# A fixed order for the opening and the first block of a linear-attention and two-MLP kernel

## The chip, the cores and the metric

The program runs on one core of a Trainium2 chip. The metric is the device time of one execution in microseconds (us), here the median of three runs. Engines are named as the profile names them: PE (TensorE, matmuls), DVE (VectorE), ACT (ScalarE), POOL (GpSimd), and SP, whose queue issues all DMAs of this kernel. Each engine carries out its own instructions strictly in the order in which they were built and waits on semaphores for the others.

## What is computed

Three stages follow each other: a gated linear attention over 4 batches, 8 heads, 768 tokens and 48 features per head, an MLP with a sigmoid gate, and an MLP with `h - tanh(h)`. Each MLP takes 3072 tokens from 384 features to 2048 and back.

```python
def _attn_ref(q, k, v, alpha):
    B, H, S, D = q.shape
    state = np.zeros((B, H, D, D), dtype=np.float32)
    y = np.zeros_like(q)
    for t in range(S):
        state = alpha[:, :, t, :, None] * state + np.einsum('bhd,bhe->bhde', k[:, :, t], v[:, :, t])
        y[:, :, t] = np.einsum('bhd,bhde->bhe', q[:, :, t], state)
    return y.astype(np.float32)
def _moe_ref(x, w_in, w_out):
    h = x @ w_in
    g = h * (1.0 / (1.0 + np.exp(-1.702 * h)))
    return (g @ w_out).astype(np.float32)
def _moe2_ref(x, w_in, w_out):
    h = x @ w_in
    g = h - np.tanh(h)
    return (g @ w_out).astype(np.float32)
```

The weights arrive as 64-bit floating-point numbers, and the kernel turns them into pairs of 32-bit numbers itself.

## The kernel before

**Attention** is done in 24 chunks of 128 tokens, numbered g, six per batch. For one chunk:

- `a_load(g)`: four DMAs (five for chunk 0) bring decay factors, keys, queries and values, 1.1 MB, into `arena` (chunks take turns in two places; chunk 2 has a third one in `gt` and `xs`).
- `prep(g, 0..3)`: two scans on DVE (L237) with a reciprocal between them, two multiplications that scale keys and queries (L243, L244), and a square of the decay factors on ACT that serves a guard (`a_guard`, L248). The square overwrites what it reads.
- `a_scores(g, x)`: eight score matmuls in two halves (L273), copied from the PSUM banks by ACT (L278, L286) and masked by POOL (L283, for chunks under `FULL` = 8).
- `a_out(g)`: eight matmuls with the carried state (L302), eight with the values (L305), eight for the new state (L312), then the state's update on DVE (L316 to L319).
- `a_evac(g)`: ACT copies the result y from PSUM to `ys` (L326), four DMAs write it to `xt` in DRAM (L331), one DMA reads it back with features on the partitions (`xlo`, L332), ACT rounds it to `xhi` (L333), and DVE (POOL from chunk 8 on) subtracts to leave the low half in `xlo` (L334).

**The MLPs** work in blocks of 512 tokens, six for each layer, with 16 steps m in a block, one for each 128 hidden features. Step s does nine matmuls into a hidden bank (`gemm1`, L343: three 128-feature parts, each as high x high, low x high and high x low), the activation (for layer 1 a tanh on ACT, L357, and a DVE instruction, L358, together `sig_1`), the split of the result into `ghi` (ACT, L361) and `glo` (DVE or POOL, L362), and three steps later nine matmuls into the output banks (`gemm2`, L350). Two hidden banks are used in turn. Block 0 needs the y of chunks 0 to 3. During each layer-1 block the chunks of the next block are worked off (`attend`).

**The weights** of layer 1 are 16 tiles of 768 KB. For each, `w_load` is one DMA into one of three `raw` buffers; `w_bits` is two DVE instructions (L160, L161), `w_join` one (L173), and `w_split` is an ACT cast to `whi` (L190) and a DVE subtraction to `wlo` (L191). `conv(1)` does a split, a join and a pair of bits for three successive tiles, and the join sets off the load of the tile three further on. There are five buffers `cf`/`xs` for tiles between bits and split.

**What sets the order.** The code is written out in one order, but the tile framework puts the instructions of each engine into an order of its own, by dependencies and by its own reckoning of times. In the opening the code calls all four parts of chunks 0 to 3 and three `conv(1)`; in block 0 each step calls `gemm1`, `sig_1`, `g_split` of the step before, the due parts of `attend` and one `conv(1)`. What runs when, DVE's order of weight conversions and chunk work above all, is the framework's choice.

## Time and profile before

| | us |
|---|---|
| median of 3 runs (lowest 973.59, highest 977.31) | 974.5 |
| the profiled execution, its own time | 975.3 |
| its span from first to last instruction | 973.2 |
| PE busy (share of the span) | 940.9 (97%) |
| DVE busy | 606.0 (62%) |
| ACT busy | 460.6 (47%) |
| POOL busy | 191.7 (20%) |

PE is near full over the whole span, but the page's 40 slices of 24.3 us show that its first four are not (5, 9, 6 and 8 tenths), while DVE is at 7, 9, 8 and 9 tenths in them and the DMA engines at 9, 7, 9 and 5. The table is read by stage: the opening up to the first MLP matmul, block 0, and the rest. The difference of 2.1 us between the execution's own time and its span lies around the first and the last instruction.

### The profile page before, as it was taken

The page shows a single profiled execution, that of the slowest core. Times are in us where ns is not written, and L with a number is a line of the kernel's source. Part 1 is how long each engine was busy: PE and PEld are TensorE (multiplying, and loading weights), DVE is VectorE, ACT ScalarE, POOL GpSimd, SP SyncE. Part 2 cuts the span into 40 slices and gives each one's busy share as a digit, 9 for nine tenths or more (in the row PEclk, how much of TensorE's full clock was granted, in tenths as well). Part 3 has the DMA queues.
Part 4 walks back from the last instruction along what each step waited for, and adds up shares of the span by engine and source line. Part 5 has one row for each costly group of instructions (what it writes and reads, how often), then busy time and mean ns, then how long its engine had stood idle before and what let it go on. Part 6 is the DMA issues. An engine that isn't in the chain of part 4 may idle for free.

```text
span 973.2 us, 13227 instructions
## 1 busy us (share of the span) xinstructions
PE 940.9 (97%) x4870; PEld 739.7 (76%) x4870; DVE 606.0 (62%) x914; ACT 460.6 (47%) x969; POOL 191.7 (20%) x150
## 2 busy tenths in 40 slices
PE   5968999999999999999999999999999999999997
PEld 4646787777777777777788888888888888888885
DVE  7989742442343453453339996766777777766663
ACT  4445434333443534434344555554556656545542
POOL 1222202434434434334230110100100101000000
PEclk9999999999999999999999999999999999999999
DMA  9795221432445463761324330100233420000001
GB/s 282 245 305 166 85 53 28 131 92 67 137 141 153 151 205 116 247 196 41 92 71 158 134 130 1 65 33 0 70 126 98 161 100 0 33 1 1 33 0 37
DMA packets 58043, 101.84 MB, mean 105 GB/s; under 512 B 4992, under 2 KB 37376, under 8 KB 57968
## 3 DMA queue, kind: packets, MB, share of 16 engines
q1 hardware_dynamic: 57968, 100.90, 32.6%
q8 instruction: 40, 0.66, 0.3%
q14 instruction: 35, 0.29, 0.1%
HBM read 86.73 MB, written 14.16 MB: 104 GB/s over the span
## 4 chain that ended last, share of the span: by engine, by line
PE 87%; DMA 5%; DVE 5%; issue 1%; ACT 1%; SPq 0%; POOL 0%; DVEq 0%; ACTq 0%
PE bank L350 40%; PE bank L343 40%; DMA arena<-xq 4%; PE bank L273 3%; PE bank L305 2%; DMA raw<-w 2%; DVE arena L237 1%; PE bank L302 1%; PE bank L312 1%; DVE cf L161 1%; DVE cf L173 1%; DVE wlo L191 0%; DVE cf L160 0%; DVE xs L173 0%; ACT arena L248 0%
## 5 line engine op out<-in xcount | busy, mean ns | idle before, releaser
L343 PE MATMUL bank<-xhi,whi 128*128 128x512 f32 x576 | 230.0, 400 | 0.2 <-ACT xhi L333 0.2
L343 PE MATMUL bank<-xlo,whi 128*128 128x512 f32 x576 | 229.8, 399 | 0.0
L343 PE MATMUL bank<-xhi,wlo 128*128 128x512 f32 x576 | 229.0, 398 | 0.0
L350 PE MATMUL bank<-ghi,whi 128*128 128x512 f32 x576 | 229.0, 398 | 0.0
L350 PE MATMUL bank<-ghi,wlo 128*128 128x512 f32 x576 | 228.5, 397 | 0.0
L350 PE MATMUL bank<-glo,whi 128*128 128x512 f32 x576 | 223.8, 396 | 0.0
L361 ACT CAST ghi<-gt 128x512 fp32r<-128x512 f32 x192 | 119.0, 620 | 199.2 <-DVE gt L373 124.1
L358 DVE SCALAR_TENSOR_TENSOR gt<-gt,bank 128x512 f32<-128x512 f32 x96 | 65.5, 682 | 125.8 <-ACT gt L357 122.7
L362 DVE TENSOR_TENSOR glo<-gt,ghi 128x512 fp32r<-128x512 f32 x128 | 93.2, 728 | 79.4 <-ACT ghi L361 76.0
L343 PEld LDWEIGHTS bank<-xhi,whi 128*128 128x128 f32 x576 | 109.0, 189 | 27.4 <-issue 1.6
L343 PEld LDWEIGHTS bank<-xlo,whi 128*128 128x128 f32 x576 | 109.1, 189 | 26.2 <-issue 1.4
L343 PEld LDWEIGHTS bank<-xhi,wlo 128*128 128x128 f32 x576 | 109.2, 190 | 25.7 <-issue 0.6
L350 PEld LDWEIGHTS bank<-ghi,whi 128*128 128x128 f32 x576 | 108.5, 188 | 26.4 <-issue 1.2
L350 PEld LDWEIGHTS bank<-ghi,wlo 128*128 128x128 f32 x576 | 108.5, 188 | 25.4 <-issue 0.8
L350 PEld LDWEIGHTS bank<-glo,whi 128*128 128x128 f32 x576 | 108.3, 188 | 25.1 <-DVE arena L243 0.2
L362 POOL TENSOR_TENSOR glo<-gt,ghi 128x512 fp32r<-128x512 f32 x64 | 85.8, 1341 | 139.0 <-ACT ghi L361 127.8
L410 POOL TENSOR_TENSOR xlo<-arena,xhi 128x512 fp32r<-128x512 f32 x18 | 27.9, 1574 | 307.6 <-ACT xhi L409 307.6
L357 ACT ACTIVATE gt<-bank 128x512 f32<-128x512 f32 x96 | 57.1, 595 | 64.0 <-PE bank L343 63.1
L237 DVE TENSOR_TENSOR_SCAN arena<-arena,seg 112x516 f32<-112x516 f32 x46 | 62.8, 1365 | 35.4 <-DMA arena<-xq 34.7
L371 DVE SCALAR_TENSOR_TENSOR arena<-arena,bank 128x512 f32<-128x512 f32 x96 | 65.7, 685 | 30.4 <-ACT arena L369 29.7
L369 ACT ACTIVATE arena<-bank 128x512 f32<-128x512 f32 x96 | 57.3, 597 | 42.2 <-PE bank L343 41.9
L373 DVE SCALAR_TENSOR_TENSOR gt<-arena 128x512 f32<-128x512 f32 x96 | 68.3, 711 | 9.4
(85 smaller groups left out, 853.7 us busy)
## 6 DMA issues: line engine op xcount, KB each, us to landing
raw<-w SPq DMA_DIRECT2D x64, 768.0 KB, 4.7
arena<-xq SPq DMA_DIRECT2D x46, 224.0 KB, 3.0
arena<-xq SPq DMA_DIRECT2D x22, 451.5 KB, 5.8
xt<-arena SPq DMA_DIRECT2D x96, 48.0 KB, 3.0
xlo<-xt SPq DMA_DIRECT2D x24, 192.0 KB, 4.1
x1t<-xs SPq DMA_DIRECT2D x6, 768.0 KB, 5.2
arena<-x1t SPq DMA_DIRECT2D x6, 768.0 KB, 4.6
out<-xs SPq DMA_DIRECT2D x18, 256.0 KB, 2.3
```

The costliest lines, as they stand in the source:

```text
L237: V.tensor_tensor_scan(out=dec(g, n), data0=src(g, n), data1=seg, initial=0.0, op0=ALU.mult, op1=ALU.max)
L273: P.matmul(out=o[hh][:, i], lhsT=k[r, 2 * x + i], rhs=q[r, 2 * x + i], start=True, stop=True)
L343: P.matmul(out=h, lhsT=w[m][:, ws], rhs=x[:, k, :n], start=c == 0, stop=c == 3 * KT - 1)
L350: P.matmul(out=acc[k][:, :n], lhsT=w[m][:, ws], rhs=x[s % 3][:, :n], start=m == 0 and c == 0, stop=m == MT - 1 and c == 2)
L357: A.activation(out=th[i][:, :n], in_=h, func=AF.Tanh, scale=0.851)
L358: V.scalar_tensor_tensor(out=gf[i][:, :n], in0=th[i][:, :n], scalar=1.0, in1=h, op0=ALU.add, op1=ALU.mult)
L361: A.copy(ghi[s % 3][:, :n], gf[s % 2][:, :n])
L362: e.tensor_tensor(out=glo[s % 3][:, :n], in0=gf[s % 2][:, :n], in1=ghi[s % 3][:, :n].bitcast(F32), op=ALU.subtract)
L369: A.activation(out=u, in_=h, func=AF.Square, accum_out=usum[:, s - NS1 :][:, :1])
L371: V.scalar_tensor_tensor(out=p, in0=u, scalar=P3, in1=h, op0=ALU.mult, op1=ALU.mult)
L373: V.scalar_tensor_tensor(out=gf[i], in0=w, scalar=PD, in1=p, op0=ALU.add, op1=ALU.mult)
L410: G.tensor_tensor(out=xlo[i][:, k], in0=xr[:, k], in1=xhi[i][:, k].bitcast(F32), op=ALU.subtract)
```

## The change

The opening is written out by hand, block 0 is rewritten in the same way, and `in_order`, called after the last step of block 0, ties every instruction of an engine to the one in front of it in the code, so that the framework keeps the written order for all that was built up to there. From block 1 on the code and its ordering are as before. Within the written order:

- Loads: values of chunk 0 come behind the decay factors of chunk 1, both first weight tiles behind the loads of chunk 2, and each later chunk load behind the y writes of the chunk that freed its place. `conv` no longer issues a weight load itself: it notes it in `due`, and `fetch()` issues it at a chosen place.
- The y of even and odd chunks goes through two buffers (`ysb`; the second shares storage with `wt`, which the weight check uses later). The read-back of y (`a_back`) stands behind the y writes of the next chunk in the opening; the rounding and subtraction (`a_x`) come a chunk or more later.
- Chunks 0 to 3 have score banks 5, 6 and 3, 4 and output banks 0, 1, which are cleared at the start; the matmuls with the carried state come behind those with the values (chunks 0 to 3).
- In the opening five tiles get their bits, four their join and three their split. In block 0 a step calls `gemm1`, one `conv(1)`, the split of `g` of the step before, a part of a chunk (a chunk takes three steps), and then `sig_1`. The guard's square comes one step later.

```diff
+        early = g < L1[0][1] // C
+        if c and not early:
+            carried(True)
         for p, hh in heads:
...
+        if c and early:
+            carried(False)
...
+    def a_back(g):
+        _, xl, o = a_at(g)
+        tk = slice(g * C, g * C + C)
         SP.dma_start(out=xl[:, :, o].bitcast(F32), in_=xt.rearrange("h d t -> (h d) t")[:, tk].rearrange("(k p) t -> p k t", p=128))
...
+    def fetch():
+        while due:
+            w_load(*due.pop(0))
...
             if m + 3 < MT:
-                w_load(layer, m + 3)
+                due.append((layer, m + 3))
...
+    def a_done(g, b=5):
+        a_evac(g, b)
+        if g + 2 < NG:
+            a_load(g + 2)
+        if g < FULL:
+            a_back(g)
...
+    def in_order(since):
+        last = {}
+        for ins in nc.cur_bb.bb.instructions[since:]:
+            if ins.engine in last:
+                tc.add_manual_dep(ins, last[ins.engine], mybir.DependencyInfo(
+                    mybir.DependencyClass.NoSync, mybir.DependencyReason.DATA), reason="in_order")
+            last[ins.engine] = ins.name
...
+    for g in range(4):
+        if g > 1:
             conv(1)
+        for r in range(2):
+            a_scores(g, r, (5, 3)[r])
+        if g < 3:
+            for r in range(3):
+                prep(g + 1, r)
+        else:
+            prep(4, 0)
+            prep(4, 1)
+        if g == 1:
+            conv(1)
+        if g > 1:
+            a_x(g - 2)
+        a_guard(g)
+        a_out(g, 0)
+        a_state(g)
+        a_evac(g, 0)
+        if g == 0:
+            a_load(3)
+            w_load(1, 2)
+        if g:
+            a_back(g - 1)
+        fetch()
+        if g == 1:
+            a_load(4)
+    a_back(3)
+    conv(1)
+    a_x(2)
+    a_x(3)
+    fetch()
+    a_load(5)
+    conv(1)
+    prep(4, 2)
+    prep(4, 3)
...
             gemm1(i, m, h, n)
-            if l == 1:
+            if l == 1 and j:
                 sig_1(s, h, n)
-            else:
+            elif l == 1:
+                conv(1)
+                fetch()
+            if l == 2:
                 tanh_near(s, h)
...
             if l == 1 and j == 0:
-                conv(1)
+                sig_1(s, h, n)
+                if m % 3 == 2 and m < 12:
+                    a_done(m // 3 + 4)
+                    a_state(m // 3 + 4)
+                if m % 3 == 0 and 0 < m < 13:
+                    prep(m // 3 + 4, 3)
+                if m % 3 == 1 and m > 3:
+                    a_x(m // 3 + 3)
...
+        if s == MT - 1:
+            in_order(begin)
```

Three places show what the table of calls does to the engines. In the rows a line number, the operation, the tile written and the tiles read stand in this order; the number behind `wlo`, `whi` or `bank` is that of the weight tile or bank, and the one behind the underscore tells nothing.

DVE before, the seven instructions up to the fourth subtraction of L334 (chunk 3), which completes the input of block 0; the split of weight tile 6 among them is the ninth split so far:

```order
L161 SCALAR_TENSOR_TENSOR cf0_101<-raw1_96,cf0_101 128x768
L237 SCALAR_TENSOR_TENSOR arena_122<-arena_122,seg_123 112x516
L191 TENSOR_TENSOR wlo6_85<-cf1_102,whi6_69 128x768
L173 SCALAR_TENSOR_TENSOR cf0_101<-raw1_96,cf0_101 128x768
L316 TENSOR_TENSOR state_121<-bank7_131,state_121 112x192
L244 TENSOR_TENSOR arena_122<-arena_122 112x4x128
L334 TENSOR_TENSOR xlo0_106<-xlo0_106,xhi0_104 128x3x128
```

DVE after, the same place, where the subtraction is L364 and stands for chunks 1, 2 and 3, the split is L192, the join L174, the bits L161 and L162:

```order
L364 TENSOR_TENSOR xlo0_105<-xlo0_105,xhi0_103 128x3x128
L333 TENSOR_TENSOR state_120<-bank7_130,state_120 112x192
L334 TENSOR_TENSOR state_120<-state_120,arena_121 112x192
L192 TENSOR_TENSOR wlo1_80<-cf1_101,whi1_64 128x768
L174 SCALAR_TENSOR_TENSOR cf2_102<-raw2_97,cf2_102 128x768
L161 TENSOR_SCALAR xs_114<-raw0_95 128x768
L162 SCALAR_TENSOR_TENSOR xs_114<-raw0_95,xs_114 128x768
L364 TENSOR_TENSOR xlo0_105<-xlo0_105,xhi0_103 128x3x128 x2
L192 TENSOR_TENSOR wlo2_81<-cf2_102,whi2_65 128x768
```

Two splits (tiles 0 and 1) now stand ahead of that subtraction instead of nine, three joins and four pairs of bits; the rest moved behind it, into block 0.

DVE before, from the first `sig_1` of block 0 (L358) to the first `glo` (L362):

```order
L358 SCALAR_TENSOR_TENSOR gt_108<-gt_108,bank3_127 128x512
L161 SCALAR_TENSOR_TENSOR xs_115<-raw1_96,xs_115 128x768
L191 TENSOR_TENSOR wlo11_90<-cf1_102,whi11_74 128x768
L244 TENSOR_TENSOR arena_122<-arena_122 112x4x128
L236 MEMSET seg_123 112x4
L191 TENSOR_TENSOR wlo9_88<-xs_115,whi9_72 128x768
L358 SCALAR_TENSOR_TENSOR gt_108<-gt_108,bank4_128 128x512
L173 SCALAR_TENSOR_TENSOR xs_115<-raw1_96,xs_115 128x768
L362 TENSOR_TENSOR glo0_112<-gt_108,ghi0_109 128x512
```

DVE after, from the first `sig_1` (L388) to the second; `glo` is L392, the scan L241:

```order
L388 SCALAR_TENSOR_TENSOR gt_107<-gt_107,bank3_126 128x512
L192 TENSOR_TENSOR wlo4_83<-xs_114,whi4_67 128x768
L174 SCALAR_TENSOR_TENSOR cf0_100<-raw2_97,cf0_100 128x768
L161 TENSOR_SCALAR cf1_101<-raw0_95 128x768
L162 SCALAR_TENSOR_TENSOR cf1_101<-raw0_95,cf1_101 128x768
L392 TENSOR_TENSOR glo0_111<-gt_107,ghi0_108 128x512
L241 SCALAR_TENSOR_TENSOR arena_121<-arena_121,seg_122 112x516
L388 SCALAR_TENSOR_TENSOR gt_107<-gt_107,bank4_127 128x512
```

Before, tiles 9 and 11 were split next to the first `sig_1`; now it is tile 4, and each step of block 0 has one split, one join, one pair of bits, one `glo`, a part of a chunk and one `sig_1`.

SP's queue before, from the y writes of chunk 0 (L331) to the read-back of chunk 1 (the second L332); L153 is a weight load, L230 to L232 are chunk loads:

```order
L331 DMA xt_133<-arena_122 48x2x128 x4
L153 DMA raw1_96<-w1 128x1536
L230 DMA arena_122<-xq 112x512
L231 DMA arena_122<-xq 112x4x128
L153 DMA raw2_97<-w1 128x1536
L332 DMA xlo0_106<-xt_133 128x3x128
L331 DMA xt_133<-arena_122 48x2x128 x4
L232 DMA arena_122<-xv 128x384
L332 DMA xlo0_106<-xt_133 128x3x128
```

SP's queue after, from the load of weight tile 2 (L154) to the read-back of chunk 1 (the second L359); y writes are L346, chunk loads L230 to L236:

```order
L154 DMA raw2_97<-w1 128x1536
L346 DMA xt_132<-wtb_98 48x2x128 x4
L359 DMA xlo0_105<-xt_132 128x3x128
L230 DMA arena_121<-xq 112x1032
L232 DMA arena_121<-xq 112x512
L234 DMA arena_121<-xq 112x4x128
L236 DMA arena_121<-xv 128x384
L346 DMA xt_132<-arena_121 48x2x128 x4
L359 DMA xlo0_105<-xt_132 128x3x128
```

Before, two weight loads and half a chunk load stand between the y writes of chunk 0 and their read-back. Now the y writes of the next chunk stand directly in front of each read-back, and a whole chunk load follows it ahead of the next y writes; the weight tile stands in front of them.

## Rows read from the trace of the kernel before

**Rows 1.** Windows by stage: busy us (instructions) of each engine, PE clock, DMA share, GB/s.

```profile
0.00:65.50 65.50, 46.33 (x304) 34.34 (x305) 57.29 (x86) 29.17 (x79) 14.20 (x14) 1.00 0.89 274
65.50:108.24 42.74, 38.41 (x196) 27.01 (x197) 41.46 (x60) 20.38 (x47) 10.59 (x6) 0.92 0.54 166
108.24:150.35 42.11, 42.11 (x227) 33.19 (x226) 21.88 (x35) 16.74 (x36) 3.66 (x4) 1.00 0.22 62
150.35:973.20 822.85, 814.03 (x4146) 645.17 (x4144) 485.32 (x735) 394.28 (x809) 163.22 (x126) 1.00 0.28 90
```

**Rows 2.** Timeline of PE: start us, us, engine, line, operation, tiles, shapes, count [idle before].

```profile
8.72 4.05 PE L273 MATMUL bank<-arena 48*128 48x176 f32 x16 [8.72 <-ACT arena L218]
...
62.33 1.11 PE L302 MATMUL bank<-arena,state 48*48 48x128 f32 x16 [1.73 <-DVE state L317]
...
65.50 1.03 PE L343 MATMUL bank<-xhi,whi 128*128 128x512 f32 x2 [0.18 <-ACT xhi L333]
...
71.52 0.63 PE L343 MATMUL bank<-xhi,wlo 128*128 128x512 f32 x1
71.94 0.63 PE L343 MATMUL bank<-xlo,whi 128*128 128x512 f32 x1
...
108.24 0.40 PE L343 MATMUL bank<-xhi,whi 128*128 128x512 f32 x1
...
146.18 0.40 PE L343 MATMUL bank<-xhi,whi 128*128 128x512 f32 x1
...
150.35 0.39 PE L343 MATMUL bank<-xhi,whi 128*128 128x512 f32 x1
```

**Rows 3.** Timeline of ACT in the opening, same columns.

```profile
19.83 0.63 ACT L326 COPY arena<-bank 112x256 f32<-112x256 f32 x2
...
56.02 0.64 ACT L326 COPY arena<-bank 112x256 f32<-112x256 f32 x2
...
64.94 0.51 ACT L333 CAST xhi<-xlo 128x384 fp32r<-128x384 f32 x1 [1.01 <-DMA xlo<-xt]
```

**Rows 4.** Timeline of DVE, same columns.

```profile
4.33 1.23 DVE L237 TENSOR_TENSOR_SCAN arena<-arena,seg 112x516 f32<-112x516 f32 x1 [2.00 <-DMA arena<-xq]
...
7.56 0.68 DVE L244 TENSOR_TENSOR arena<-arena 112x512 f32<-112x512 f32 x1
...
47.18 0.54 DVE L160 TENSOR_SCALAR cf<-raw 128x768 int32<-128x768 int32 x1
...
56.86 0.95 DVE L161 SCALAR_TENSOR_TENSOR cf<-raw,cf 128x768 int32<-128x768 int32 x1
57.73 0.55 DVE L334 TENSOR_TENSOR xlo<-xlo,xhi 128x384 fp32r<-128x384 f32 x1
58.20 0.35 DVE L316 TENSOR_TENSOR state<-bank,state 112x192 f32<-112x192 f32 x1
...
82.06 0.68 DVE L358 SCALAR_TENSOR_TENSOR gt<-gt,bank 128x512 f32<-128x512 f32 x1
82.66 0.95 DVE L173 SCALAR_TENSOR_TENSOR xs<-raw,xs 128x768 int32<-128x768 int32 x1
83.53 0.68 DVE L362 TENSOR_TENSOR glo<-gt,ghi 128x512 fp32r<-128x512 f32 x1
84.13 1.22 DVE L237 TENSOR_TENSOR_SCAN arena<-arena,seg 112x516 f32<-112x516 f32 x1
85.27 0.53 DVE L160 TENSOR_SCALAR cf<-raw 128x768 int32<-128x768 int32 x1
```

**Rows 5.** Groups by line and shape, first 180 us: mean ns, idle before. POOL's mask.

```profile
L283 POOL TENSOR_SCALAR_AFFINE_SELECT arena<-arena 128x512 f32<-128x512 f32 x16 | 22.9, 1440 | 90.4 <-ACT arena L278 77.0 <-ACT arena L286 13.4
```

**Rows 6.** Timeline of POOL and DVE where both work at once.

```profile
44.95 5.60 POOL L283 TENSOR_SCALAR_AFFINE_SELECT arena<-arena 128x512 f32<-128x512 f32 x2 [6.99 <-ACT arena L278]
...
107.00 1.94 DVE L173 SCALAR_TENSOR_TENSOR cf<-raw,cf 128x768 int32<-128x768 int32 x1
```

**Rows 7.** Waits of the first 110 us: who waited for whom, us, times, longest.

```profile
ACT xhi L333 <- DMA xlo<-xt: 11.0, 6, 3.0
```

More of the change, by code (lines that the diff above doesn't have):

```diff
@@ L296, in at, with carried @@
             return y[hh][64 * (p % 2) : 64 * (p % 2) + D, p // 2]
-        if c:
+        def carried(start):
             for p in range(NP):
@@ L301, in a_out @@
                     r = slice(64 * hh, 64 * hh + D)
-                    P.matmul(out=at(p, hh), lhsT=state[r, p], rhs=q[r, p, :C], start=p < 2, stop=False)
+                    P.matmul(out=at(p, hh), lhsT=state[r, p], rhs=q[r, p, :C], start=start and p < 2, stop=not start and p >= 2)
+        early = g < L1[0][1] // C
+        if c and not early:
+            carried(True)
         for p, hh in heads:
@@ L305, in a_out @@
             P.matmul(out=at(p, hh), lhsT=vt(g)[:, p, D * hh : D * hh + D], rhs=s4[:, hh, p % 2],
-                     start=not c and p < 2, stop=p >= 2)
+                     start=(early or not c) and p < 2, stop=not (c and early) and p >= 2)
+        if c and early:
+            carried(False)
         if c < NCH - 1:
@@ L321, in a_evac @@
     def a_evac(g, b):
[L322 to L324 removed]
+        ys = ysb[g % 2 if g < FULL else 0]
         for hh in range(2):
@@ L455, in linear_attention_mlps @@
+    begin = len(nc.cur_bb.bb.instructions)
     V.memset(seg, A_MIN)
-    a_load(0)
+    a_load(0, (0, 1, 2, 3))
     SP.dma_start(out=cs, in_=cst)
-    a_load(1)
+    a_load(1, (0, 1))
+    a_load(0, (4,))
+    a_load(1, (2, 3, 4))
+    a_load(2)
+    w_load(1, 0)
+    w_load(1, 1)
+    for b in (0, 1, 7):
+        V.memset(bank[b], 0.0)
+    V.memset(state, 0.0)
     for g in range(3):
         eye(g)
-    w_load(1, 0)
-    w_load(1, 1)
-    a_load(2)
-    w_load(1, 2)
-    a_scan(0, 0)
-    a_scan(0, 1)
```

73 lines of the change are left out of this document (43 added, 30 removed).

## The prediction

> **What bounds the kernel now.** I read the page first, then the windows by stage, then the timelines of PE, ACT, DVE and SP in the first 150 us. The page shows PE at 97%, but that is a mean over stages. Three marks on PE's timeline cut the part that the change touches [rows 2]: the first gemm1 of block 0 starts at 65.50, the eighth (tile 7) at 108.24, the first gemm1 of block 1 at 150.35. From 65.50 to 108.24 seven steps take 42.74 us, 6.1 each; from 108.24 to 150.35 nine take 42.11, 4.7 each, with PE never idle [rows 1]. A bare step, with no chunk work in it, is 150.35 - 146.18 = 4.17 [rows 2].
>
> The windows tell who is the bound in each stretch [rows 1]. Up to 65.50 DVE is busy 57.29 of 65.50 us, the DMA engines 89%, PE 46.33 and mostly with small attention matmuls. From 65.50 to 108.24 DVE is busy 41.46 of 42.74: it is the bound, and PE waits now and then. After 108.24 DVE is at half and PE is full. So the kernel is bound first by a chain through all engines with a nearly full DVE, then by DVE, then by PE until the end. After 150.35 the change leaves code and (but for a few rows of the last block) PE's order as they were, so 822.85 us stay.
>
> What does DVE do before 65.50? The order shows it: nine weight tiles are split before block 0's input is complete, and tile 11 is next to the first `sig_1`, where only tile 0 and 1 are needed. DVE is full with work that PE wants 20 to 40 us later, while the chain that lets PE start (scores, y, write, read-back, xhi) takes 12 us per chunk: y of chunk 0 leaves PSUM at 19.83, that of chunk 3 at 56.02 [rows 3]. From there it is 9.5 us to the first gemm1, by way of the write and the read-back: xhi of chunk 3 starts at 64.94, gemm1 at 65.50 [rows 2, 3].
>
> **The change part by part.** No arithmetic is removed; three bank clears replace one, two more of about 0.5 us on DVE ahead of the first scan at 4.33, where it waits 2.00 us for its load [rows 4]: free. All the rest is order.
>
> *The opening.* Chunk 0 is prepared as before, from 4.33 to 8.2 on DVE [rows 4]. Its eight score matmuls take 4.05 us [rows 2], then come ACT's copies (about 0.6), POOL's mask (1.44 mean, [rows 5]) and the rest of the output matmuls (about 0.6): y of chunk 0 leaves at about 15.5 (before 19.83). Now the chunks follow each other without conversions between: scores 3.2 to 4.05, copies 0.6, mask of the second half 1.44, carried state 1.1 (its L302 row, [rows 2]), and, judged by that row, 0.5 to 1.0 for the second half of the values and 0.7 to 1.2 for the new state. That is 7.5 to 9.4 us; I take 8, since two score matmuls of different row halves alternate now. DVE's part per chunk (4.1 us preparation, as chunk 0's 3.9) and one bundle of conversion fit beside it. So y of chunk 3 leaves at 15.5 + 3 x 8 = 39.5. Add 9.5 as before, less 1 because DVE is free for the last subtraction: the first gemm1 at **48**. Bounds: 45 (7 us a chunk, copies hidden beside the masks) and 55 (9.4, and 3 us by read-backs that hold ACT in front of y).
>
> *SP.* By 48 us the loads in front of the last read-back are five chunks (1.1 MB), five weight tiles (0.79 MB) and y both ways (0.2 MB each), some 11 MB; at the 274 GB/s of the opening [rows 1] that is 40 us, so DMA is near but not over. In block 0 a step needs 0.77 MB of weights and a third of 1.5 MB of chunk and y, 1.3 MB in 6 us or 211 GB/s: below 274. A weight load is issued two steps (12 us) ahead of its bits. I cost SP at nothing; if this cover fails, DVE waits in order with everything behind it (the third rival).
>
> *Block 0 on DVE.* Each step now has on DVE, start to start [rows 4]: split 0.87 (as join), join 0.87, bits 0.47 + 0.87 and 0.1 because the second needs the first, glo 0.60, sig_1 0.60: 4.4. A chunk per three steps adds two scans 2.3, the reciprocal and clear 0.2, scaling 1.2, subtraction 0.47, state 0.6: 4.8, or 1.6 a step. Sum 6.0, and 0.1 for instructions stretched while POOL works: 6.1. PE's part is 4.2 + 3.4/3 (a chunk's matmuls at full clock) = 5.3, so DVE stays the bound until the conversions are through. From the first gemm1 DVE has 9.5 us until sig_1 of step 0 is out (splits of tiles 2 and 3, two joins, two pairs of bits, scaling, a scan, sig_1), then ten steps to sig_1 of step 10: 48 + 9.5 + 61 = 118.5. Conversion then ends, and PE may run: gemm1 of steps 12 to 15 and gemm2 of 9 to 12 are eight times 2.1 us, and 1.2 for the handover: 18. Block 1's first gemm1 would be at **136.5** instead of 150.35, a gain of 13.9.
>
> Why not more: DVE's work is the same. Before, it has 98.75 us of it in the 108.24 us up to the eighth step [rows 1]; the change only lets PE take its steps while DVE converts, instead of afterwards. Why not less: before, PE takes eight full steps after DVE is through; now four.
>
> *The guard's square* moves on ACT behind sig_1 of the next step. ACT is 45% busy [rows 1]; nothing on PE waits for the square but the load that reuses its place, six steps later. Nothing.
>
> *A place where the skill speaks against the change.* POOL's mask stands twice in each chunk's chain. Its mean is 1.44 [rows 5], but two masks at 44.95 took 5.60 together while DVE ran one conversion behind the other, and a DVE join took 1.94 instead of 0.95 beside POOL [rows 4, 6]. The Trainium skill's SBUF — State Buffer (section SBUF: two separate sides) says that a DVE instruction with two SBUF inputs and a POOL instruction that reads SBUF exclude each other for their whole length. By that rule masks in a chain beside gapless scans are the rule's worst case; the rows bear it out for some masks, while the mean says that most get through. By the rule each mask would take 2.8 and the sum would be the second rival's.
>
> **The sum.** Own time 975.3 (span 973.2 and 2.1 around it) - 13.9 = 961.4. The median of the runs is 974.5, 0.8 below that execution. Forecast **961**. With the start at 45 and 5.9 a step it is 956; with 55 and 6.3 a step 971.
>
> **The rivals.**
>
> *PE is the bound from the start.* If DVE's steps were not binding (its stalls gone and conversions ahead), block 0 would last 16 x 4.17 and four chunks of 3.4, less three gemm2 of 2.1, plus 4 at the lower clock: 78 us from 46, mark at 124, gain 26: **949**. Against it stands the sum of DVE above.
>
> *The opening stays slow.* Eight masks at 2.8 instead of 1.44 add 11 us: first gemm1 at 59, mark at 147.5, **972 to 973**. For it stands [rows 6]; against it the mean, and that DVE has idle time in the new opening. It decides if masks average over 2.3.
>
> *The read-back holds ACT: slower.* ACT now carries out xhi at a fixed place, with whi casts, tanh and y copies behind it. Before, it waited for the read-back six times, 11.0 us in all, longest 3.0 [rows 7], with the framework putting other work in front. If each of seven read-backs (chunks 0 to 6) comes 3.5 us late and DVE, waiting for whi in order, loses the same, that is 24 us: **985**. It decides at 2 us lost per chunk, where the gain of 13.9 is gone. Against it: a read-back in block 0 has two steps (12 us) from y to xhi, and the whole way took 9 us before, 56.02 to 64.94 [rows 3].
>
> *The lower clock.* Early matmuls of 512 columns follow each other at 0.42 us (71.52 to 71.94, [rows 2]), which is 1.2 GHz, the later ones take 4.17/18 = 0.23; the mean granted share of 65.50 to 108.24 is 0.92 and after that 1.00 [rows 1]. If PE, which now waits for DVE in every third step, stayed at 1.2 GHz through twelve steps, a step would be 18 x 0.42 + 2.2 = 9.8 and the mark 48 + 117.6 + 17 = 182.6: **1008**. The Trainium skill's TensorE: Matmul & The Clock Gate (section Why this matters for your kernels) asks for no long idle gaps between matmul bursts. Against it: a slow PE would itself be the bound and so be busy without gaps, and after such a run of unbroken matmuls the clock came back here, since the mean of that stretch is 0.92 and not 0.5 [rows 1].
>
> **How the numbers follow.** Forecast 961: 0.74. Slow opening, 972: 0.12, half of it within 0.5% (4.9 us) of 974.5, half faster. PE-bound, 949: 0.04. Read-back, 985: 0.07. Clock, 1008: 0.03. A difference of less than 0.5% can hardly be told from none here. Faster 0.74 + 0.04 + 0.06 = 0.84, within 0.06, slower 0.10. The range takes the forecast's bounds and the slow opening: 952 to 972.
>
> **What would show it.** First gemm1 near 48 and y of chunks about 8 us apart; two splits before it; block 0's steps at about 6.1 us with DVE over 90% busy up to about 118; the first gemm1 of block 1 near 136, and everything behind it shifted by the same amount. The forecast is wrong if the first gemm1 is after 58 (the chain was not shortened), if DVE has idle pieces over 1 us in most steps of block 0 (read-back or weights), or if what is gained by 136 is given back in later blocks.

## The result and the profile after

The changed kernel takes 965.15 us (median of four, 964.48 to 968.22), the kernel before, run beside it, 974.16. The ratio is 0.991, 95% interval 0.988 to 0.994: faster by 9 us. The forecast was 961 with 952 to 972, so the range held and the forecast itself was 4 us low. The profiled execution of the changed kernel has a span of 966.2 us and an own time of 968.22, the longest of its four; the rows below come from it, so they show a gain of 7.0 us where the medians show 9.0.

Windows of the kernel after, cut at the first gemm1 of block 0, the eleventh step ([rows 1] was cut at the eighth) and the first gemm1 of block 1, called the "mark" from here on; columns as in [rows 1]:

```profile
0.00:48.41 48.41, 25.90 (x240) 19.80 (x240) 36.64 (x57) 21.06 (x62) 9.34 (x12) 1.00 0.86 242
48.41:112.25 63.84, 54.51 (x322) 40.55 (x322) 61.11 (x86) 30.83 (x73) 8.82 (x7) 0.92 0.67 207
112.25:142.75 30.50, 28.79 (x165) 22.35 (x164) 27.17 (x39) 12.90 (x27) 7.50 (x6) 1.00 0.36 90
142.75:966.20 823.45, 815.22 (x4146) 646.10 (x4144) 486.42 (x736) 393.74 (x809) 165.84 (x126) 1.00 0.28 90
```

PE starts 17.1 us earlier, but the mark comes only 7.6 us earlier (142.75 against 150.35): block 0, which took 84.85 us, now takes 94.34, because DVE (the fourth figure, 61.11 of 63.84 us) now does there the conversions that it used to do before PE's start. Behind the mark the length is the same within 0.6 us, so nothing was given back later.

PE's timeline after, to be read against [rows 2]: block 0's first gemm1, the third, steps 14 and 15, and the mark. Behind the row stands what ended PE's idle time.

```profile
48.41 0.79 PE L373 MATMUL bank<-xhi,whi 128*128 128x512 f32 x1 [8.60 <-ACT xhi L363]
...
61.42 0.79 PE L373 MATMUL bank<-xhi,whi 128*128 128x512 f32 x1 [3.80 <-DVE gt L388]
...
133.34 0.50 PE L373 MATMUL bank<-xhi,whi 128*128 128x512 f32 x1 [1.04 <-DVE gt L388]
...
138.46 0.50 PE L373 MATMUL bank<-xhi,whi 128*128 128x512 f32 x1 [0.67 <-DVE gt L388]
...
142.75 0.39 PE L373 MATMUL bank<-xhi,whi 128*128 128x512 f32 x1
```

ACT's timeline after, against [rows 3]: the four copies of y (L341), the last cast of x (L363), and what stands around chunk 4's guard square (L252):

```profile
14.56 0.80 ACT L341 COPY arena<-bank 112x256 f32<-112x256 f32 x2 [0.57 <-PE bank L313]
...
22.46 0.65 ACT L341 COPY wtb<-bank 112x256 f32<-112x256 f32 x2 [2.17 <-PE bank L306]
...
31.20 0.51 ACT L363 CAST xhi<-xlo 128x384 fp32r<-128x384 f32 x1 [4.31 <-DMA xlo<-xt]
...
32.68 0.62 ACT L341 COPY arena<-bank 112x256 f32<-112x256 f32 x2
...
39.33 0.62 ACT L341 COPY wtb<-bank 112x256 f32<-112x256 f32 x2
...
47.85 0.51 ACT L363 CAST xhi<-xlo 128x384 fp32r<-128x384 f32 x1 [2.64 <-DMA xlo<-xt]
...
53.66 1.06 ACT L252 ACTIVATE arena<-arena 112x1032 f32<-112x1032 f32 x1 [4.56 <-DVE arena L248]
...
54.72 0.82 ACT L191 CAST whi<-xs 128x768 fp32r<-128x768 f32 x1
```

DVE's timeline after: two idle pieces around PE's start, the first and the eleventh sig_1 (L388), and the scans (L241) of block 1's chunk 9 among block 0's last sig_1:

```profile
48.39 0.56 DVE L364 TENSOR_TENSOR xlo<-xlo,xhi 128x384 fp32r<-128x384 f32 x1 [2.59 <-ACT xhi L363]
...
55.57 0.96 DVE L192 TENSOR_TENSOR wlo<-xs,whi 128x768 fp32r<-128x768 f32 x1 [1.95 <-ACT whi L191]
...
60.71 0.66 DVE L388 SCALAR_TENSOR_TENSOR gt<-gt,bank 128x512 f32<-128x512 f32 x1
...
122.36 0.66 DVE L388 SCALAR_TENSOR_TENSOR gt<-gt,bank 128x512 f32<-128x512 f32 x1
...
131.47 1.23 DVE L241 TENSOR_TENSOR_SCAN arena<-arena,seg 112x516 f32<-112x516 f32 x1 [2.27 <-DMA arena<-xq]
132.62 0.66 DVE L388 SCALAR_TENSOR_TENSOR gt<-gt,bank 128x512 f32<-128x512 f32 x1
```

What the opening waits for has changed too. `--critical` follows the chain of work that ended last back through the trace and gives each line's share of a stretch; its summary line up to block 0's first gemm1 (the view cuts it at its end), before and then after:

```profile
by line: DMA arena<-xq 26.5%; DMA raw<-w 23.0%; DVE cf L161 6.9%; DVE arena L237 5.9%; issue 5.0%; DVE cf L160 4.9%; DVE cf L173 4.8%; DVE wlo L191 4.0%; DVE xs L173 2.9%; DVE xlo L334 2.1%; ACT arena L248 1.8%; DVE xs L161 1.5%; DVE arena 
```

```profile
by line: DMA cs<-cst 12.2%; PE bank L277 11.9%; PE bank L313 8.9%; DMA xlo<-xt 8.8%; POOL arena L287 8.3%; issue 5.7%; ACT whi L191 4.8%; PE bank L322 4.7%; ACT arena L282 4.6%; PE bank L306 4.3%; DMA xt<-wtb 3.5%; ACT arena L219 2.9%; DVE 
```

Before, half of the chain is loads of chunks (`xq`) and weights (`w`) and a quarter is DVE's conversions (L160, L161, L173, L191). After, it begins with the load of constants (`cst`) and runs through the scores, masks, output matmuls and one read-back; no load of a chunk or a weight tile stands in it.

### The profile page after: what moved, and what is told of

It is laid out like the page before. It is cut to its first block, busy times and chain, and to the rows that moved or that the text cites. A ratio compares the mean times of both kernels' runs of the same rounds, so it can differ in the third digit from the quotient of the medians.

```text
span 966.2 us, 13208 instructions
## 1 busy us (share of the span) xinstructions
PE 924.4 (96%) x4870; PEld 728.8 (75%) x4870; DVE 611.3 (63%) x916; ACT 458.5 (47%) x969; POOL 191.5 (20%) x150
## 4 chain that ended last, share of the span: by engine, by line
PE 83%; DVE 7%; DMA 4%; issue 1%; ACT 1%; SPq 1%; POOL 0%; DVEq 0%; ACTq 0%
PE bank L380 38%; PE bank L373 38%; PE bank L277 3%; DMA arena<-xq 3%; PE bank L313 2%; DVE arena L241 2%; DVE wlo L192 1%; PE bank L306 1%; PE bank L322 1%; DVE glo L392 1%; SPq L346 1%; DVE cf L174 1%; DMA cs<-cst 1%; DVE gt L388 1%; DVE xs L174 0%
## 5 line engine op out<-in xcount | busy, mean ns | idle before, releaser
L392 DVE TENSOR_TENSOR glo<-gt,ghi 128x512 fp32r<-128x512 f32 x128 | 93.1, 727 | 74.3 <-ACT ghi L391 71.0
L388 DVE SCALAR_TENSOR_TENSOR gt<-gt,bank 128x512 f32<-128x512 f32 x96 | 65.3, 680 | 118.1 <-ACT gt L387 105.9
L392 POOL TENSOR_TENSOR glo<-gt,ghi 128x512 fp32r<-128x512 f32 x64 | 87.5, 1368 | 122.2 <-ACT ghi L391 111.3
L241 DVE TENSOR_TENSOR_SCAN arena<-arena,seg 112x516 f32<-112x516 f32 x46 | 64.0, 1390 | 35.3 <-DMA arena<-xq 34.2
L399 ACT ACTIVATE arena<-bank 128x512 f32<-128x512 f32 x96 | 57.3, 597 | 42.2 <-PE bank L373 41.8
```

What stands on the lines that cost most here:

```text
L241: V.tensor_tensor_scan(out=dec(g, n), data0=src(g, n), data1=seg, initial=0.0, op0=ALU.mult, op1=ALU.max)
L388: V.scalar_tensor_tensor(out=gf[i][:, :n], in0=th[i][:, :n], scalar=1.0, in1=h, op0=ALU.add, op1=ALU.mult)
L392: e.tensor_tensor(out=glo[s % 3][:, :n], in0=gf[s % 2][:, :n], in1=ghi[s % 3][:, :n].bitcast(F32), op=ALU.subtract)
L399: A.activation(out=u, in_=h, func=AF.Square, accum_out=usum[:, s - NS1 :][:, :1])
```

## The experiments

All edits are to the changed kernel unless said otherwise. "Start" is block 0's first gemm1, "block 0" the time from there to the mark, "behind" the rest of the span; the ratio is that to the kernel before, run on the same chip.

| kernel | start | mark | block 0 | behind | median us | ratio (95%) |
|---|---|---|---|---|---|---|
| before | 65.5 | 150.4 | 84.9 | 822.9 | 974.2 | |
| after | 48.4 | 142.8 | 94.3 | 823.5 | 965.2 | 0.991 (0.988 to 0.994) |
| e1_no_tie | 69.4 | 151.2 | 81.8 | 821.8 | 974.1 | 1.000 (0.998 to 1.002) |
| e2_tie_opening | 46.4 | 139.3 | 92.9 | 823.2 | 967.3 | 0.994 (0.991 to 0.996) |
| e3_guard_later | 47.3 | 139.5 | 92.2 | 822.7 | 962.1 | 0.988 (0.985 to 0.990) |
| e4_hold_scans | 46.9 | 140.4 | 93.5 | 822.5 | 964.1 | 0.990 (0.987 to 0.992) |
| e5_tie_before | 73.6 | | | | 1048.4 | 1.076 (1.073 to 1.079) |
| e6_less_bits | 47.5 | 134.1 | 86.6 | | | |
| e7_mask_twice | 57.3 | 151.2 | 93.9 | 823.8 | 977.0 | one run |
| e8_glo_pool | 47.4 | 144.8 | 97.5 | 821.1 | 967.8 | 0.995 (0.992 to 0.997) |
| e9_guard_hold | 47.0 | 138.3 | 91.3 | 823.8 | 962.3 | 0.986 (0.984 to 0.988) |
| e10_fill | 47.4 | 135.7 | 88.3 | 823.5 | 959.2 | 0.983 (0.980 to 0.985) |
| e11_guard_step | 47.6 | 152.2 | 104.6 | 823.4 | 974.9 | 1.000 (0.999 to 1.002) |
| e12_loads_first | 49.5 | 143.0 | 93.6 | 820.6 | 965.8 | 0.992 (0.991 to 0.994) |

The start varies by two microseconds between kernels whose opening is the same (46.4 to 48.4), so block 0's length tells small effects better than the mark. DVE's part of it repeats more closely: from the start to the beginning of the first sig_1 it is 12.29 or 12.30 us in the kernel after and in e4, e7, e8, e11 and e12, which leave that way alone, and the ten steps behind it are 61.6 or 61.7 us in the kernel after and in e3, e4, e7, e9 and e12.

### What makes the gain: the order, or holding to it

**e1_no_tie.**

```diff
-        if s == MT - 1:
-            in_order(begin)
```

> The changed kernel without its last edit: the instructions up to the end of block 0 are written in the new order, but are no longer tied to one another on each engine, so that the framework places them by its own priorities (on DVE conversions of weights then stand among the opening's scans and state updates, on PE the state products stand in front of the scores' followers). Theory (the tie makes the gain: it keeps the opening's chain free of conversions): the first gemm1, at 48.4 us in the changed kernel and at 65.5 before, comes at 54 to 66, and the time is 969 to 976 us. Rival (the rewritten text and the order of the loads make it, the tie adds nothing): the first gemm1 at 48 to 50 and 964 to 967 us.

The theory held, and beyond its range at the start: 69.4 us, 3.9 later than before, and not 54 to 66. No gain is left. DVE's timeline of e1 shows what came back, by its splits (L192) among the subtractions of x (L364):

```profile
47.19 0.54 DVE L364 TENSOR_TENSOR xlo<-xlo,xhi 128x384 fp32r<-128x384 f32 x1
48.67 0.95 DVE L192 TENSOR_TENSOR wlo<-cf,whi 128x768 fp32r<-128x768 f32 x1
...
54.46 0.95 DVE L192 TENSOR_TENSOR wlo<-cf,whi 128x768 fp32r<-128x768 f32 x1
...
59.40 0.56 DVE L364 TENSOR_TENSOR xlo<-xlo,xhi 128x384 fp32r<-128x384 f32 x1
```

The same text, left to the framework, has conversions between the chunks again: nine splits stand ahead of the fourth subtraction (at 70.50), as many as in the kernel before, against two in the kernel after.

**e2_tie_opening.** The call moves to the end of the opening.

```diff
     prep(4, 2)
     prep(4, 3)
+    in_order(begin)
...
-        if s == MT - 1:
-            in_order(begin)
```

> The tie covers the opening alone (to the second half of chunk 4's preparation); block 0's sixteen steps are placed by the framework. The first gemm1 should come at 48 to 49 as in the changed kernel. Theory (the gain is the earlier start; behind it DVE's work sets the pace whatever the order, since DVE is busy in 14.8 of each 15 us from 75 to 120): block 1's first gemm1 at 141 to 146, against 142.75, and 964 to 969 us. Rival (in block 0 it is the order that holds the gain, since without it conversions and followers of the attention change places on PE and DVE): block 1's first gemm1 at 148 or later and 971 us or more.

The mark came at 139.3, earlier than the theory's 141 to 146, with the start at 46.4; the time lies in its range. Block 0 took 92.9 us in the framework's order and 94.3 in the written one, and the intervals of the two ratios overlap. The tie earns its gain in the opening; the tie over block 0 earns nothing that these runs can show.

**e5_tie_before.** The kernel before, with nothing changed but the tie.

```diff
+    begin = len(nc.cur_bb.bb.instructions)
     V.memset(seg, A_MIN)
...
+        if s == MT - 1:
+            in_order(begin)
```

> The kernel before with the tie alone: up to the end of block 0 each engine keeps the order in which before's code is written; order of the code and loads are those of before. Theory (the tie makes the gain only together with the order that the change writes): in before's written order ACT's cast of a chunk's x stands right behind that chunk's copy of y, so ACT waits out each way through memory (3.0 to 11.0 us by the rows of before and after) before the next chunk's copies, and each step's sig_1 stands on DVE ahead of that step's conversions, so that DVE waits for PE in every step; the first gemm1 no earlier than 60 us, steps of 7 us or more, 980 to 1010 us. Rival (any fixed order does it, since it keeps the framework from putting conversions in front of the chain): the first gemm1 at 50 us or earlier, 962 to 970 us.

The theory's side, and worse than its range: 7.6% slower. ACT's waits in e5, up to 160 us (total, times, longest):

```profile
ACT gt L357 <- PE bank L343: 41.0, 8, 7.2
ACT xhi L333 <- DMA xlo<-xt: 34.3, 6, 6.5
ACT arena L248 <- DVE arena L244: 18.0, 4, 6.0
```

So neither half makes the gain alone. Two waits of ACT stand out: the tanh waits until PE is through, with all later work of ACT behind it (41.0 us), and the cast of x until the read-back is in (34.3 us in six). The second is the mechanism of the prediction's third rival, at 5.7 us a chunk, and it reaches PE: PE's longest waits in block 0, 7.37, 7.68 and 7.33 us (ending at 107.95, 133.73 and 161.73), are for weight casts that stand behind such a wait on ACT. How much the first wait costs is not shown.

What these three runs do not separate is the parts of the written order. In the chain of before the loads weigh more than the conversions, and no run moves the conversions alone back into the opening or restores the old order of the loads alone; e12 below changes only their place against the writes of y.

### What sets block 0's pace

**e6_less_bits.** With 1 as its third argument `w_bits` issues only the first of its two instructions, for tiles 5 to 15. This sends the program into its general path at the end (12,039 us), so only the first 150 us are read; line numbers are one higher there.

```diff
-            w_bits(layer, cv[0] % MT)
+            w_bits(layer, cv[0] % MT, 1 if 4 < cv[0] < MT else 2)
```

> The changed kernel with one of the four conversion instructions left out for the weight tiles 5 to 15 of layer 1: the one that puts the sign into the assembled value (0.96 us on DVE each, 11 of them, 10.5 us in all), so these weights lose their sign. Theory (in block 0 DVE sets the pace, as the sum had it with 6.1 us a step): the ten steps from the first to the eleventh sig_1 take 52 to 56 us instead of 61.7, and block 1's first gemm1 stands 84 to 89 us behind block 0's first one instead of 94.3; 955 to 960 us. Rival (PE, or the chunks' loads, set the pace beside it): the ten steps 59 us or more, block 1's first gemm1 92 us or more behind, 963 us or more.

The first and the eleventh sig_1 of e6 on DVE:

```profile
58.74 0.66 DVE L389 SCALAR_TENSOR_TENSOR gt<-gt,bank 128x512 f32<-128x512 f32 x1
...
114.08 0.65 DVE L389 SCALAR_TENSOR_TENSOR gt<-gt,bank 128x512 f32<-128x512 f32 x1
```

Ten steps took 55.3 us instead of 61.65 and block 0 86.6 instead of 94.3, both within the theory's figures. DVE sets the pace. The next limit stands close behind it: in those ten steps DVE, which never waited there in the kernel after, now waited three times for the load of a chunk (1.48, 2.22 and 1.56 us, ending at 73.93, 91.04 and 107.75), so less came out (6.3 us) than was taken away (ten instructions of 0.87 us or more).

**e8_glo_pool.**

```diff
-                prev = s - 1, n, V if l == 2 or j in (0, len(L1) - 1) else G
+                prev = s - 1, n, V if l == 2 or j == len(L1) - 1 else G
```

> The changed kernel with block 0's low halves of g (16 instructions, 0.69 to 0.76 us each on DVE, 11 to 12 us in all) on POOL instead of DVE, as in the blocks behind it, where POOL takes 1.37 us each; POOL was busy 16 of 94 us in block 0. Theory (DVE sets block 0's pace): the ten steps take 53 to 57 us instead of 61.7, block 1's first gemm1 stands 86 to 91 us behind the first gemm1 instead of 94.3, 957 to 961 us. Rival (POOL's work lengthens DVE's beside it, or PE sets the pace): the ten steps 60 us or more, 963 to 966 us.

The theory's price failed, though its premise stands by e6. DVE lost its low halves and the ten steps took 64.8 us (59.66 to 124.42), 3.1 more. One step of e8, DVE first, then POOL:

```profile
106.73 0.94 DVE L174 SCALAR_TENSOR_TENSOR cf<-raw,cf 128x768 int32<-128x768 int32 x1
107.59 0.55 DVE L161 TENSOR_SCALAR xs<-raw 128x768 int32<-128x768 int32 x1
108.17 1.94 DVE L162 SCALAR_TENSOR_TENSOR xs<-raw,xs 128x768 int32<-128x768 int32 x1
```

```profile
106.26 3.03 POOL L392 TENSOR_TENSOR glo<-gt,ghi 128x512 fp32r<-128x512 f32 x1 [3.33 <-ACT ghi L391]
```

The second bits instruction takes 1.94 us instead of 0.96 and ends 0.8 us after POOL does, as if it began then; POOL's subtraction takes 3.03, with the join inside it. Each held up the other, and what DVE gave away it lost in longer instructions: over the ten steps the second bits instructions took 5.9 us more, the first ones 2.9 and the scans 1.3, against 7.8 us of subtractions that had left.

### The two places where the sum was short

**e3_guard_later.**

```diff
     prep(4, 2)
-    prep(4, 3)
...
-                if m % 3 == 0 and 0 < m < 13:
+                if m % 3 == 0 and m < 13:
```

> Chunk 4's guard square on ACT leaves the opening and is issued behind the first step's tanh. In the changed kernel it stood at 53.66 behind a wait of 4.56 us for DVE, the weight cast of tile 3 stood behind it at 54.72, and DVE waited 1.95 us for that cast at 55.57. Theory (this is the greater part of the 3.4 us by which the way from the first gemm1 to the first sig_1 was forecast too short, and DVE has no other slack up to 129 us): the first sig_1 on DVE at 58.3 to 59.2 instead of 60.71, block 1's first gemm1 1.5 to 2.2 us earlier (140.5 to 141.3), 963 to 964 us. Rival (PE or a load takes the place of the wait, the gain is lost by the end of block 0): the first sig_1 earlier, block 1's first gemm1 within 0.7 us of 142.75, 965 us.

```profile
52.39 0.95 DVE L192 TENSOR_TENSOR wlo<-xs,whi 128x768 fp32r<-128x768 f32 x1
...
57.39 0.66 DVE L388 SCALAR_TENSOR_TENSOR gt<-gt,bank 128x512 f32<-128x512 f32 x1
```

In these two rows of DVE of e3 the split no longer waits, and the first sig_1 starts 10.1 us behind PE's start instead of 12.3. Block 0 is 2.1 us shorter, the median 3 us. The theory held; the absolute times lie one lower than forecast, since this run's start was at 47.3. The intervals of the two ratios (0.985 to 0.990 and 0.988 to 0.994) overlap, so it is the trace that shows the 2.1 us.

**e4_hold_scans.**

```diff
         if s == MT - 1:
             in_order(begin)
+            tied = len(nc.cur_bb.bb.instructions)
+        if s == MT + 3:
+            ins = nc.cur_bb.bb.instructions
+            end = [q for q in ins[begin:tied] if q.engine == mybir.EngineType.DVE][-1]
+            for q in ins[tied:]:
+                if q.engine == mybir.EngineType.DVE:
+                    tc.add_manual_dep(q, end.name, mybir.DependencyInfo(
+                        mybir.DependencyClass.NoSync, mybir.DependencyReason.DATA), reason="hold")
```

> DVE's instructions of block 1 (the scans of chunk 9 among them) may no longer be placed in front of block 0's last sig_1; nothing else is changed. In the changed kernel four scans stand among the last sig_1 from 131.47 on, the first of them behind a load that landed late (2.27 us of DVE idle), and PE waited 1.04 and 0.67 us for sig_1 in front of the steps 14 and 15. Theory (these scans are what made the end of block 0 longer than its 18 us): both waits of PE gone, block 1's first gemm1 1.5 to 2.5 us earlier (140.2 to 141.3), 963 to 964 us. Rival (the scans are then late for block 1, which gives the gain back, or the waits stay because DVE's conversions end them): block 1's first gemm1 within 0.5 us of 142.75 or the time behind it longer than 823.5 us by as much, 965 us.

Both waits of PE are gone (steps 14 and 15 start at 132.0 and 136.2, and from step 13 on steps are 4.2 us apart), but block 0 is only 0.8 us shorter: step 10 started at the same 112.2 us in spite of a start 1.5 us earlier. The windows of 105 to 120 us, first of the kernel after, then of e4 (the share ahead of the last two figures is PE's granted clock), show where it was lost:

```profile
105.00:120.00 15.00, 13.11 (x78) 9.81 (x77) 14.83 (x23) 8.05 (x20) 4.00 (x3) 1.00 0.56 155
```

```profile
105.00:120.00 15.00, 13.10 (x71) 9.68 (x70) 14.86 (x21) 6.99 (x18) 4.64 (x3) 0.89 0.58 155
```

For a part of that stretch PE ran at the lower of its two levels, 1.2 GHz, after an idle piece of 1.90 us that ended at 107.61, while in the kernel after an idle piece of 1.89 us that ended at 109.26 had no such result. In e7, e9 and e12 an idle piece of 1.90 us at this place was followed by the lower level as in e4 (granted clock 0.50 in 119.5 to 122.5, 107.0 to 110.3 and 112.0 to 115.0). From that idle piece to the mark PE of e4 has no further gap, so the slow piece counts in full: 32.8 us, against 33.5 in the kernel after, of which 1.7 are its two waits. From step 10 to the mark e4 needs 28.2 us against 30.5. So the end is shorter by what was said, the total is not, and 964.1 against 965.2 decides nothing.

**e9_guard_hold.** Both edits.

> The changed kernel with both edits together: chunk 4's guard square behind the first step's tanh, and DVE's instructions of block 1 behind block 0's last sig_1. Alone, the first gave 962.1 us (block 1's first gemm1 92.2 us behind block 0's first one, against 94.3), the second 964.1 us (93.5). Theory (both are waits at different ends of the same row of DVE work, so they add): 91 to 91.8 us behind the first gemm1, 960.5 to 962 us. Rival (PE, without a wait for sig_1 from step 10 on once the scans are held, sets the end of block 0): 92.2 or more, 962 to 964 us.

Block 0 took 91.3 us, as the theory had it (0.9 less than e3); the median, 962.3, is the rival's. By time the second edit cannot be told from nothing.

**e10_fill.** On top of e9:

```diff
     a_x(2)
+    prep(4, 2)
+    w_split(1, cv[2])
+    cv[2] += 1
     a_x(3)
     fetch()
     a_load(5)
-    conv(1)
-    prep(4, 2)
+    conv(1, False)
```

> The kernel of the run above (guard square later, scans held) with three instructions written elsewhere: DVE's scaling of chunk 4 and the split of weight tile 2 (with its cast on ACT) move in front of the last chunk's x. In the changed kernel DVE stood idle for 2.59 us at 45.24 to 48.39, waiting for that x to come back from memory, with the scaling (1.3 us) and the split (0.95 us) behind it. Theory (from about 12 us to the end of block 0 the sum of DVE's work and its idle time sets the time, so filling an idle stretch of the opening shortens the whole by as much, though no part of the path to the first gemm1 is touched): the idle stretch down to 0.3 us or less, the first gemm1 where it was (47 to 48.5), the first sig_1 1.8 to 2.5 us earlier measured from the first gemm1, 958 to 960.5 us. Rival (the time goes by when PE starts; work moved within the wait changes nothing): within 0.7 us of the run above.

DVE's timeline of e10 at the place where it stood idle for 2.59 us:

```profile
43.83 0.55 DVE L364 TENSOR_TENSOR xlo<-xlo,xhi 128x384 fp32r<-128x384 f32 x1
44.30 0.69 DVE L247 TENSOR_TENSOR arena<-arena 112x512 f32<-112x512 f32 x1
...
45.51 0.95 DVE L192 TENSOR_TENSOR wlo<-cf,whi 128x768 fp32r<-128x768 f32 x1
47.36 0.56 DVE L364 TENSOR_TENSOR xlo<-xlo,xhi 128x384 fp32r<-128x384 f32 x1 [0.91 <-ACT xhi L363]
...
54.88 0.66 DVE L388 SCALAR_TENSOR_TENSOR gt<-gt,bank 128x512 f32<-128x512 f32 x1
```

The start stayed (47.4), 0.91 us of the gap were left and not 0.3, the first sig_1 came 7.5 us behind the start instead of e9's 10.1, block 0 took 88.3 us and the median is 959.2: the theory's figure, 3.1 us below e9. This version beats both kernels of the study.

But only half of block 0's 3.0 us came by the theory's way. DVE's ten steps took 62.7 us instead of 61.6, so that sig_1 of step 10 was 1.5 us ahead of e9's and no longer 2.6. The other 1.5 us lie in PE's last stretch without a gap, from its last wait to the mark, the same work in both (first e9, then e10; the share ahead of the last two figures is the granted clock):

```profile
105.56:138.34 32.78, 32.78 (x182) 26.02 (x182) 25.49 (x37) 15.62 (x34) 5.81 (x4) 0.95 0.41 114
```

```profile
104.44:135.67 31.23, 31.23 (x181) 24.91 (x182) 25.32 (x37) 15.34 (x34) 5.94 (x4) 1.00 0.44 119
```

PE's wait ahead of that stretch was 1.90 us in e9 and 0.37 in e10, and in e9 alone the granted clock fell behind it. The theory had no such term.

### Other parts of the change

**e7_mask_twice.**

```diff
-            G.affine_select(out=s3, in_=s3, pattern=[[0, 4], [1, C]], channel_multiplier=1, base=1 - C,
-                            compare_op=ALU.is_ge, fill=0.0)
+            for _ in range(2 if g < 4 else 1):
+                G.affine_select(out=s3, in_=s3, pattern=[[0, 4], [1, C]], channel_multiplier=1, base=1 - C,
+                                compare_op=ALU.is_ge, fill=0.0)
```

> The changed kernel with the mask of the scores on POOL issued twice for the chunks 0 to 3 (eight more instructions of 0.73 to 1.40 us in the opening; the result is the same). It measures whether the mask lies on the opening's chain, on which the rival of a slow opening rested. Theory (it does: PE waits for the mask in front of every chunk's value product, 0.2 to 1.6 us by the rows of the changed kernel): about one further mask for each of the chunks 0, 1 and 3 and two for chunk 2 is seen, the first gemm1 at 52 to 57 instead of 48.4, 969 to 973 us. Rival (the way through memory and the loads hide it): the first gemm1 within 1.5 us of 48.4, 964 to 967 us.

POOL's masks of chunk 2 in the kernel after (count and time of both together; the eight of chunks 0 to 3 sum to 9.15 us):

```profile
25.56 2.80 POOL L287 TENSOR_SCALAR_AFFINE_SELECT arena<-arena 128x512 f32<-128x512 f32 x2 [5.33 <-ACT arena L282]
```

and in e7 (the sixteen sum to 20.80):

```profile
29.48 5.39 POOL L288 TENSOR_SCALAR_AFFINE_SELECT arena<-arena 128x512 f32<-128x512 f32 x4 [5.29 <-ACT arena L282]
```

11.7 us more of masks moved the start by 8.9 us and the mark by 8.4: about three quarters of the added time reached PE's start, which with 57.3 lies just past the theory's 52 to 57, and the one run's 977.0 us lies past its 969 to 973. Block 0 does not make it good.

**e11_guard_step.** Here the square overwrites decay factors that the state update of the same step still reads, so the states built from them are other than the reference's.

```diff
-        if 0 < r < 3 or r == 3 and g >= FULL:
+        if r:
             prep(g + 1, r)
...
-                if m % 3 == 0 and 0 < m < 13:
-                    prep(m // 3 + 4, 3)
```

> The changed kernel with the third edit of the change undone: the guard squares of the chunks 5 to 8 on ACT in the step in which the chunk's scaling on DVE ends, ahead of that step's tanh, and not one step later. Theory (ACT then waits for DVE's scaling, and the tanh that stands behind it holds sig_1; four places, 1 to 2 us each, by the row at 53.66 where a guard square waited 4.56 us): block 1's first gemm1 96 to 101 us behind the first one instead of 94.3, 967 to 972 us. Rival (ACT has room enough, idle half of the time in block 0): within 0.7 us of 94.3, 964.5 to 966 us.

ACT's and PE's waits in e11, 48 to 160 us:

```profile
ACT arena L252 <- DVE arena L248: 18.5, 4, 4.8
```

```profile
PE bank L277 <- ACT arena L341: 7.7, 2, 3.9
PE bank L277 <- ACT wtb L341: 2.5, 1, 2.5
```

The theory held and was too small: block 0 took 104.6 us, all of the gain lost. ACT's square waits for DVE's scaling (three places besides chunk 4's), and behind it stand the tanh and the copy of y whose bank PE wants for the next scores. DVE waited three times 1.71 us for that tanh (up to 73.15, 94.93 and 116.80), which it does nowhere in block 0 of the kernel after.

**e12_loads_first.**

```diff
-        a_evac(g, 0)
         if g == 0:
             a_load(3)
             w_load(1, 2)
-        if g:
-            a_back(g - 1)
         fetch()
         if g == 1:
             a_load(4)
+        a_evac(g, 0)
+        if g:
+            a_back(g - 1)
```

`a_done` has its load in front of `a_evac` too, for chunks under `FULL`.

> The changed kernel with one part undone: on SP the loads of later chunks and weight tiles stand ahead of a chunk's writes of y, in the opening and in block 0, and no longer behind them; nothing else is moved. Some of these loads wait for a buffer of the chunk that is just ending (the load at 23.44 us did, and the writes of y of chunk 1, which ACT had ready at 23.1, left SP at 24.97 behind it). Theory (SP is one queue; a load that waits for its buffer holds the writes behind it, ACT's cast of chunk 0's x waits longer for the way through memory, and the copy of chunk 2's y behind that cast comes late with it): ACT's first cast of x at 35 to 38 instead of 31.2, the first gemm1 at 53 to 58 instead of 48.4, 970 to 975 us. Rival (the writes have time enough, since x is wanted only at the end of the opening): the first gemm1 at 50 or earlier, 964 to 967 us.

The rival won. ACT's timeline of e12:

```profile
33.80 0.51 ACT L363 CAST xhi<-xlo 128x384 fp32r<-128x384 f32 x1 [7.89 <-DMA xlo<-xt]
...
35.28 0.62 ACT L341 COPY arena<-bank 112x256 f32<-112x256 f32 x2
```

The read-back came 2.6 us later and held y of chunk 2 by as much, but the start came at 49.5 (48.4 in the kernel after, 46.4 to 47.6 in the others with its opening) and the time moved by nothing that can be told.

## Why the prediction was right, and where it was not

- **The opening: right.** y of the four chunks leaves at 14.56, 22.46, 32.68 and 39.33 (forecast 15.5 and every 8 us to 39.5), gemm1 at 48.41 (48). That it is so near is in part luck: chunk 0 was 0.9 us early, the three steps 0.8 longer and the way from y to gemm1 0.6 longer, and the start of kernels with this same opening scatters by two us. The steps were not equal (7.9, 10.2, 6.7): chunk 2's copy waited for a read-back (31.20, [4.31]) and chunk 3 made most of it up. e1 and e5 show that order and tie are both needed. The prediction put the old delay down to DVE's conversions; the chain of before passes through loads of chunks and weights for twice as long.
- **From the start to the first sig_1: wrong, 12.95 us instead of 9.5.** The sum listed DVE's work and left out a wait, 1.95 us for the cast behind chunk 4's guard square, which the text passed over when it costed the guard at nothing (e3 took 2.2 us away here). It also left out the last chunk's subtraction, which DVE begins only as PE starts (0.7 us, 48.39 to 49.13), and a join that took 1.38 us instead of 0.95 (at 56.45, while POOL masked). That is 3.1 of the 3.45 us. e10 did not take away an error of the sum: it put 2.1 us of the listed work ahead of the start.
- **Ten steps at 6.1: right**, 61.65 us (forecast 61) and DVE-bound (e6).
- **The end, 18 us: 19.7.** The sum took block 0 to be closed, but the tie binds only what was built up to its last step; scans of block 1 slipped in front of the last sig_1. PE waited for them 1.04 and 0.67 us, which is the excess. That removing the waits gives it back is not shown: in e4, e9 and e12, where PE did not wait, the same end took 19.0 us, since PE was still behind from the piece at the lower clock. In e10, with neither, it took 17.5, so 18 was about right for PE's own work.
- **Behind the mark: right**, 823.45 against 822.85.
- **The guard one step later at nothing: right as it stands**, but the edit is not idle: without it the gain is gone (e11).
- **SP at nothing: right.** From the start to step 10 the DMA engines moved 207 GB/s (forecast 211) and in that time DVE did not wait for a load. Even with loads in front of the writes the time stays (e12). e6 shows that there is little to spare.
- **The rivals.** PE as the bound falls with e6. A slow opening did not come, because the eight masks took 9.15 us together, 1.14 each; its mechanism is real (e7). The read-back did hold ACT, 13.1 us in four waits of the opening, but up to the last chunk little of it reached PE: from the scores of chunk 3 to its value matmuls it took 4.3 us (31.28 to 35.57), in chunks 1 and 2 3.7. In e5 it weighs. The lower clock did not stay: the granted clock was 0.92 from the start to step 10 and 1.00 behind it.
- **The range.** Its lower end, 952, follows from no term: the sum's own lower bound was 956. Its upper bound, a start at 55 and 6.3 a step, gives a mark of 145.5 and 970.5 us, not 971. Neither decides anything here.

Together: 0.4 us at the start, 3.4, 0.7 and 1.7 behind it make the 6.2 us between the mark of 136.5 and 142.75. With the 0.6 behind the mark this is the way from the 961.4 us forecast for a profiled execution to the 968.2 of the one that was profiled; the median lies 3.1 us below that one, so by the median the forecast is only 4 us low.

## What to carry to other kernels

Where one engine's row is full from the opening to the end of a stage, price its idle pieces and not only the path to the first big matmul: moving 2.1 us of work into a wait brought sig_1 of step 10 forward by 1.5 us although PE started no earlier. Before the whole gain is put down to such a move, compare the granted clock of the two runs: the other 1.5 us of that gain were PE's clock. A fixed order is as good as the order that is fixed: look on each in-order engine for an instruction that waits for another engine, and at what stands behind it. A tie over a part of a program leaves its end open to what the framework brings in from behind.

## What the runs showed of the hardware

That work moved from DVE to an idle POOL would make DVE no freer was e8's rival, not its theory. In steps 0 to 10 the second bits instruction had a mean of 1.11 to 1.19 us after and 1.71 to 1.77 in e8 (one mean for each destination, `cf` and `xs`), the first 0.55 to 0.62 and 0.83 to 0.92; splits and joins stayed at 0.95. Groups of DVE in e8, 60 to 125 us (busy us, mean ns, idle before):

```profile
L162 DVE SCALAR_TENSOR_TENSOR cf<-raw,cf 128x768 int32<-128x768 int32 x6 | 10.2, 1706 | 0.2
L192 DVE TENSOR_TENSOR wlo<-cf,whi 128x768 fp32r<-128x768 f32 x6 | 5.7, 947 | 0.0
L161 DVE TENSOR_SCALAR cf<-raw 128x768 int32<-128x768 int32 x6 | 5.5, 918 | 0.0
```

The form of the instruction alone does not decide, since the split has two SBUF inputs as the second bits instruction has and stays at 0.95. What fits is which of them meets POOL in the fixed order. The Trainium skill's SBUF — State Buffer (section SBUF: two separate sides) describes an exclusive lock, held for the whole instruction by the engine that starts first; the step of e8 shown above agrees (1.94 us on DVE is 0.82 past POOL's end; 3.03 us on POOL, 1.37 elsewhere, contains a whole join, as if POOL waited first). Why the first bits instruction, with one SBUF input, is longer too stays open here.
